# The first loads of a fused attention and MLP kernel: one chunk in two halves, two chunks on another queue, one warming matmul less

## The chip, the cores and the metric

The kernel runs on one core of a Trainium2 chip. A core has five engines that run side by side, each through its own list of instructions, in order: TensorE (PE; its weight loads are shown as PEld), VectorE (DVE), ScalarE (ACT), GpSimd (POOL) and SyncE (SP). They wait for each other by semaphores. Loads and stores are issued by an engine, SP in almost all cases here, and carried out by 16 DMA engines that the core has.

The metric is device time of one execution in microseconds (us). Durations inside the kernel come from a profile of one execution.

## The reference

The reference normalizes the rows of x (2048 tokens by 1024 columns), and adds to x an attention branch and a token-mixing MLP branch. The branch that the kernel starts with is the MLP; it normalizes the already normalized rows once more and mixes over tokens:

```python
def _B_ref(x, w1, b1, w2, b2):
    B, S, D = x.shape
    h = _layernorm(x, axis=-1)
    u = jnp.einsum('bsd,sf->bdf', h, w1) + b1
    u = _gelu(u)
    y = jnp.einsum('bdf,fs->bds', u, w2) + b2
    return (lambda x, *d: x.transpose(*d))(y, 0, 2, 1)
x = A_x
xn = _layernorm(x, axis=-1)
return x + _A_ref(xn, A_wq, A_wk, A_wv, A_wo, A_beta) + _B_ref(xn, B_w1, B_b1, B_w2, B_b2)
```

All inputs are bf16. The attention branch (32 heads, 4 segments with a memory carried from one to the next, and an output projection) is not touched by the change.

## The kernel before

x is cut into 16 chunks of 128 tokens, c=0 to c=15; a chunk is a tile of 128 partitions by 1024 columns (256 KB) in `xin`. w1 is cut the same way by token; of its 3584 columns the first 512 come first, one piece of 128 by 512 (128 KB) for each chunk, in `w1all`.

**Start.** `loads` (L761) issues the loads. POOL sets two small constants; ACT runs one activation (L765) whose only purpose is to have the table of the Gelu function loaded early; then SP issues, in this order: x chunk 0, x chunk 1, w1 piece 0, x chunk 2, x chunk 3, w1 piece 1, x chunk 4, w1 pieces 2 and 3, x chunk 5, w1 pieces 4 and 5, and from there pairs. All loads go through one helper, `dma` (L247), so all have that line in the profile. Its argument `issuer` says which engine issues; in `loads` it is SP for all.

`warm` (L800) has DVE clear a tile and PE multiply it by itself N_WARM = 12 times, with a result that nobody reads; then DVE writes the constants that the statistics need (L810).

**Statistics and first hidden units.** `norm_and_first_hidden` (L813) writes out the order by hand. For each chunk, mean and variance of its rows are found, then 1/sqrt on POOL (`scale`, L899), then `ln_h` (L907) on DVE writes the normalized chunk into `h`, as two halves of 512 columns for the first chunks. Then `early_hidden` (L912) lets PE multiply the chunk with the w1 piece: 8 matmuls of 128x128 by 128x512, for 4 blocks of hidden units and 2 halves of the columns, added up in 8 banks of PSUM over all 16 chunks. In c=0 to c=2 the four matmuls of the first half come first.

The statistics are shared out:

- c=0: DVE, `bn_stats` over columns 0 to 511 (L876), then over 512 to 1023 (L878), then `aggregate` (L885).
- c=1: `stats_halved`: the first half on DVE (L851), the second in two passes on ACT (L853, sum; L855, squares), a small step on POOL (L857), and `aggregate` on DVE.
- even chunks from c=2: two passes of ACT over the whole chunk (L869, L871).
- odd chunks from c=3: DVE, in halves as c=0.

On DVE the order at the start is: both statistics of c=0 and their aggregate, the first-half statistics of c=1, the first half of `ln_h` of c=0, the aggregate of c=1, the second half of `ln_h` of c=0, the first statistics of c=3, both halves of `ln_h` of c=1. On ACT: the two passes over c=1, then those over c=2, c=4 and so on.

**After that.** `hidden` (L982) computes the other 24 blocks of hidden units with 16 matmuls each for two halves, with w1 streamed in; the normalized x is transposed by DMA on the side. Then come attention and the rest of the MLP, in an order that a planner at build time writes out: it keeps a modelled clock for each engine (`fw.now`) and picks what to put on PE next by comparing modelled times of readiness with PE's clock.

**Waits.** Each tile or part has a resource (`Res`) that remembers who wrote and read it last; an operation waits for what it names in `reads` and `writes`. A chunk of x has one resource, `R_xin[c]`. `over_early` (L684) later reuses the space of `xin` and waits for all that read it.

Of the kernel before, what the change touches and what calls it, by code (L numbers as in the profile page):

```python
# [584 lines left out]
class _Kernel:  # L585
# [3 lines left out]
    N_SLOT = 18  # L589
    RESERVE = 60  # L590
    ACT_STATS = (2, 4, 6, 8, 10, 12, 14)
    N_WARM = 12
    C2 = LN_EPS * LN_EPS / (1.0 + LN_EPS)

    def __init__(self, nc, ctx, A_x, A_wq, A_wk, A_wv, A_wo, A_beta, B_w1, B_b1, B_w2, B_b2, out):
# [27 lines left out]
    def alloc(self):  # L623
        nc = self.nc
        a = self.keep = _Arena(nc, self.SB_BASE, self.SB_END)
        self.brow = a.take("brow", [64, P], BF16)
        self.bt = a.take("bt", [P, 64], BF16)
        self.bc = a.take("bc", [P, 64], F32)
        self.beta_sb = a.take("beta_sb", [P, N_HEAD], BF16)
        self.gcol = a.take("gcol", [P, N_HEAD], F32)  # L630
        self.gate = a.take("gate", [P, N_GRP, 2, 4], F32)
        self.eps8 = a.take("eps8", [P, 2, 4], F32)
        self.diag = a.take("diag", [P, 4, VW], F32)
        self.ln_mv = a.take("ln_mv", [P, N_TCH, 2], F32)
        self.ln_t = a.take("ln_t", [P, N_TCH, 4], F32)
        self.ln_r1 = a.take("ln_r1", [P, N_TCH], F32)
        self.ln_r2 = a.take("ln_r2", [P, N_TCH], F32)
        self.mhalf = a.take("mhalf", [P, N_TCH], F32)
        self.vA = [a.take(f"vA{i}", [P, 4, 16, VW], BF16) for i in range(2)]
        self.MZ32 = a.take("MZ32", [P, N_GRP, GW], F32)  # L640
        self.MZbf = a.take("MZbf", [P, N_GRP, GW], BF16)
        self.srec = a.take("srec", [P, 2, 32], F32)
        self.xnT = [a.take(f"xnT{s}", [P, N_DCH, SEG_L], BF16) for s in range(N_SEG)]
        self.gT = a.take("gT", [P, N_FCH, D_MODEL], BF16)
        self.b1c, self.b2c = self.bc[:, 0:32], self.bc[:, 32:64]

        self.R_brow2 = Res("brow2")
        self.R_brow, self.R_bt, self.R_bc = Res("brow"), Res("bt"), Res("bc")
        self.R_beta, self.R_gcol, self.R_gate = Res("beta"), Res("gcol"), Res("gate")
        self.R_eps, self.R_diag, self.R_mhalf = Res("eps8"), Res("diag"), Res("mhalf")  # L650
        self.R_st = [Res(f"st{c}") for c in range(N_TCH)]
        self.R_mean = [Res(f"mean{c}") for c in range(N_TCH)]
        self.R_var = [Res(f"var{c}") for c in range(N_TCH)]
        self.R_rs = [Res(f"rs{c}") for c in range(N_TCH)]
        self.R_r1 = Res("r1")
        self.R_vA = [[Res(f"vA{i}_{c}") for c in range(4)] for i in range(2)]
        self.R_MZ32 = [Res(f"mz32_{g}") for g in range(N_GRP)]
        self.R_MZbf = [Res(f"mzbf_{g}") for g in range(N_GRP)]
        self.R_srec = [Res(f"srec{i}") for i in range(2)]
        self.R_xnT = [Res(f"xnT{c}") for c in range(N_TCH)]  # L660
        self.R_gT = [[Res(f"gT{fc}_{h}") for h in range(2)] for fc in range(N_FCH)]
        self.R_out = [[Res(f"out{c}_{h}") for h in range(2)] for c in range(N_TCH)]

        self.early_base = a.at
        e = _Arena(nc, self.early_base, self.SB_END)
        self.xin = e.take("xin", [P, N_TCH, D_MODEL], BF16)
        self.xn_tmp = [e.take(f"xn_tmp{i}", [P, D_MODEL], BF16) for i in range(4)]
        self.early_end = e.at
        self.h = e.take("h", [P, N_TCH, D_MODEL], BF16)
        self.w1all = e.take("w1all", [P, 3 * N_TCH * 256], BF16)  # L670
        self.ln_st = e.take("ln_st", [P, N_TCH, 15], F32)
        self.late_end = e.at
        self.w1first = self.w1all[:, 0:N_TCH * 512].rearrange("p (c f) -> p c f", c=N_TCH)
        self.w1slot = [self.w1all[:, i * N_TCH * 256:(i + 1) * N_TCH * 256].rearrange("p (c f) -> p c f", c=N_TCH)
                       for i in range(3)]
        self.R_xin = [Res(f"xin{c}") for c in range(N_TCH)]
        self.R_xnt = [Res(f"xnt{i}") for i in range(4)]
        self.R_half = [Res(f"half{i}") for i in range(3)]
        self.R_one = Res("one")
        self.R_h = [[Res(f"h{c}_{hf}") for hf in range(2)] for c in range(N_TCH)]  # L680
        self.R_w1f = [Res(f"w1f{i}") for i in range(N_TCH)]
        self.R_w1s = [None, None, Res("w1s2")]

    def over_early(self):  # L684
        fw = self.fw
        e = _Arena(self.nc, self.early_base, self.early_end)
        wait = _after(*self.R_xin, *self.R_xnt)
        self.wv_sb = e.take("wv_sb", [P, N_DCH, D_MODEL], BF16)
        self.wqr = [e.take(f"wq{i}", [P, N_DCH, P], BF16) for i in range(2)]
        self.wkr = [e.take(f"wk{i}", [P, N_DCH, P], BF16) for i in range(2)]  # L690
        self.w2r = [e.take(f"w2n{i}", [P, 5, P], BF16) for i in range(5)]
        self.w2l = [e.take(f"w2l{i}", [P, 4, P], BF16) for i in range(4)]
        self.w2s = [e.take(f"w2s{i}", [P, P], BF16) for i in range(2)]
        self.prod = e.take("prod", [P, 4, P], BF16)
        self.R_prod = Res("prod", wait)
        self.o_s = [e.take(f"o_s{i}", [P, 4, P], BF16) for i in range(2)]
        self.R_os = [Res(f"o_s{i}", wait) for i in range(2)]
        self.R_wv = [Res(f"wv{i}", wait) for i in range(2)]
        self.R_wq = [Res(f"wq{i}", wait) for i in range(2)]
        self.R_wk = [Res(f"wk{i}", wait) for i in range(2)]  # L700
        self.R_w2 = [Res(f"w2n{i}", wait) for i in range(5)]
        self.R_w2l = [Res(f"w2l{i}", wait) for i in range(4)]
        self.R_w2s = [Res(f"w2s{i}", wait) for i in range(2)]
        self.pkT = e.take("pkT", [P, SEG_L], BF16)
        self.etmp = e.take("etmp", [P, SEG_L], BF16)
        self.R_pkT = Res("pkT", wait)
        self.R_etmp = Res("etmp", wait)
        self.wq_ring = _Ring(fw, [t[:] for t in self.wqr], self.R_wq)
        self.wk_ring = _Ring(fw, [t[:] for t in self.wkr], self.R_wk)
        for i in range(N_UNIT):  # L710
            g = i % N_GRP
            self.wq_ring.srcs.append(self.A_wq[:, g * P:(g + 1) * P].rearrange("(dc p) j -> p dc j", p=P))
            self.wk_ring.srcs.append(self.A_wk[:, g * P:(g + 1) * P].rearrange("(dc p) j -> p dc j", p=P))
        self.fill = _Fill(self)
        self.wq_ring.ensure(0)
        self.wk_ring.ensure(0)
        for bv in range(2):
            fw.dma(self.wv_sb[:, :, bv * 512:(bv + 1) * 512],
                   self.A_wv[:, bv * 512:(bv + 1) * 512].rearrange("(dc p) j -> p dc j", p=P), writes=[self.R_wv[bv]])
# [41 lines left out]
    def loads(self):  # L761
        fw = self.fw
# [1 line left out]
        fw.op("pool", lambda e: e.memset(self.brow[:], 0.0), writes=[self.R_brow, self.R_brow2])  # L764
        fw.op("act", lambda e: e.activation(self.ln_t[:, 0, 0:1], self.mhalf[:, 0:1], ACT.Gelu_apprx_tanh),  # L765
              reads=[self.R_mhalf], writes=[self.R_st[0]], ns=1500)
        self.load_x(0, 1)
        self.load_x(1, 1)
        self.load_w1(0, 1)
        self.load_x(2, 1)  # L770
        self.load_x(3, 1)
        self.load_w1(1, 1)
        self.load_x(4, 1)
        self.load_w1(2, 2)
# [2 lines left out]
        for c in range(6, 16, 2):  # L777
            self.load_x(c, 2)
            self.load_w1(c, 2)
            if c == 6:  # L780
                fw.dma(self.brow[0:N_FCH, :], self.B_b1.rearrange("(c q) -> c q", q=P), reads=[self.R_brow],
                       writes=[self.R_brow])
                fw.dma(self.brow[32:32 + N_TCH, :], self.B_b2.rearrange("(c q) -> c q", q=P), reads=[self.R_brow2],
                       writes=[self.R_brow2])
# [3 lines left out]
        fw.dma(self.w1slot[2], self.w1_srcs[2], writes=[self.R_w1s[2]])  # L788
        self.w1_next = 3

    def load_x(self, c0, n):
        self.fw.dma(self.xin[:, c0:c0 + n, :], self.x_d[:, c0:c0 + n, :],
                    writes=[self.R_xin[c] for c in range(c0, c0 + n)])

    def load_w1(self, c0, n, issuer="sp"):
        self.fw.dma(self.w1first[:, c0:c0 + n, :],
# [63 lines left out]
    def stats(self, c, part=None, whole=True):  # L860
        fw = self.fw
# [13 lines left out]
        if part != 1:  # L875
            fw.op("dve", lambda e: e.bn_stats(st[:, 0:6], src[:, 0:512]), reads=[self.R_xin[c]], writes=[R_t], ns=690)  # L876
        if part != 0:
            fw.op("dve", lambda e: e.bn_stats(st[:, 6:12], src[:, 512:1024]), reads=[self.R_xin[c], R_t], writes=[R_t],  # L878
                  ns=690)
            if whole:  # L880
                self.aggregate(c)
# [20 lines left out]
    def ln_h(self, c, half=None):  # L902
        fw = self.fw
        a, z = (0, D_MODEL) if half is None else (512 * half, 512 * half + 512)
        for hf in ((0, 1) if half is None else (half,)):
            assert self.R_h[c][hf] is not None
        fw.op("dve", lambda e: e.tensor_scalar(self.h[:, c, a:z], self.xin[:, c, a:z], self.ln_mv[:, c, 0:1],  # L907
                                               self.ln_r2[:, c:c + 1], op0=ALU.subtract, op1=ALU.mult),
              reads=[self.R_xin[c], self.R_mean[c], self.R_rs[c]],
              writes=self.R_h[c] if half is None else [self.R_h[c][half]], ns=(z - a) // 2 + 30)  # L910

    def early_hidden(self, c):  # L912
# [51 lines left out]
    def ln_xn(self, c):  # L964
        fw = self.fw
        k = c % 4
        fw.op("dve", lambda e: e.tensor_scalar(self.xn_tmp[k][:], self.xin[:, c, :], self.ln_mv[:, c, 0:1],
                                               self.ln_r1[:, c:c + 1], op0=ALU.subtract, op1=ALU.mult),
              reads=[self.R_xin[c], self.R_mean[c], self.R_r1], writes=[self.R_xnt[k]], ns=750)

    def x_transpose(self, c):
        s, cc = c // 4, c % 4
# [656 lines left out]
```

## Time and profile before

| | us |
|---|---|
| median of 5 runs | 690.8 |
| lowest and highest | 690.37, 690.84 |
| the profiled execution | 690.8 |
| its span, first to last instruction | 689.1 |

Lines of the profile give the start, the duration, the engine, the source line, the operation, `out<-in` by the program's names, shapes, and in brackets how long the engine sat idle before and what ended the wait. "SPq" and "ACTq" are the sequencers of those engines: issuing a load or waiting for a semaphore is their work and not counted as busy time. The early loads and when they land, from the DMA issues of the first 6 us (issue plus time to landing):

| load | issued by SP at | to landing | landed |
|---|---|---|---|
| x chunk 0, 256 KB | 0.81 | 2.8 | 3.6 |
| x chunk 1, 256 KB | 1.26 | 2.9 | 4.2 |
| w1 piece 0, 128 KB | 1.72 | 4.3 | 6.0 |
| x chunk 2, 256 KB | 2.19 | 4.5 | 6.7 |
| x chunk 3, 256 KB | 2.65 | 4.7 | 7.4 |
| w1 piece 1, 128 KB | 3.14 | 4.5 | 7.6 |
| x chunk 4, 256 KB | 3.61 | 4.7 | 8.3 |

### The profile page before, as it was taken

How to read it: one execution, taken by the hardware profiler on the slowest of the kernel's cores; microseconds unless marked ns; L12 is line 12 of the kernel's file. 1: busy time of each engine (PE TensorE's matmuls, PEld its weight loads, DVE VectorE, ACT ScalarE, POOL GpSimd, SP SyncE). 2: the span in 40 equal slices, each digit the busy share in tenths (PEclk: the TensorE clock that was granted, in tenths of full speed). 3: DMA queues.
4: the chain of work that ended last, by engine and by line, in shares of the span. 5: the costliest groups of instructions: out<-in, count | busy, mean ns of one | idle time of the engine just before them, and what ended most of it. 6: DMA issues, size and time to landing. Idle time of an engine off the chain costs nothing.

```text
span 689.1 us, 12060 instructions
## 1 busy us (share of the span) xinstructions
PE 679.4 (99%) x4772; PEld 327.0 (47%) x4853; DVE 235.2 (34%) x510; ACT 308.6 (45%) x611; POOL 150.1 (22%) x363
## 2 busy tenths in 40 slices
PE   8999999999999999999999999999999999999998
PEld 3444444444444454444454544544545444544554
DVE  7811100000001242434462461643536333442524
ACT  7331111111134475755645472744747443534540
POOL 4800000000001232323312231312323131312330
DMA  8367666325027656657547556474564546445334
GB/s 321 109 178 183 159 159 200 100 61 144 1 83 179 148 132 149 146 120 182 132 102 159 124 123 151 94 169 106 130 147 103 120 117 159 107 102 136 86 85 138
DMA packets 275714, 92.06 MB, mean 134 GB/s; under 512 B 234186, under 2 KB 272074, under 8 KB 275658
## 3 DMA queue, kind: packets, MB, share of 16 engines
q1 hardware_dynamic: 275658, 91.28, 53.5%
q8 instruction: 39, 0.64, 0.4%
q14 instruction: 17, 0.14, 0.1%
HBM read 74.47 MB, written 5.24 MB: 116 GB/s over the span
## 4 chain that ended last, share of the span: by engine, by line
PE 96%; DMA 1%; ACT 1%; issue 1%; DVE 0%; SPq 0%
PE ps_all L217 96%; DMA xin<-in_A_x_dram 1%; DMA w2n<-in_B_w_dram 1%; ACT pT L1161 1%; ACT xn_tmp L869 0%; DVE ost L1230 0%; SPq L247 0%; ACT xn_tmp L871 0%; DVE h L907 0%; DVE fin L1368 0%
## 5 line engine op out<-in xcount | busy, mean ns | idle before, releaser
L1169 POOL TENSOR_SCALAR_AFFINE_SELECT pT<-pT 128x256 bf16<-128x256 bf16 (+1 forms) x320 | 127.5, 408 | 508.4 <-ACT pT L1161 498.8
L1161 ACT ACTIVATE pT<-ps_all 128x512 bf16<-128x512 f32 x320 | 161.9, 618 | 76.7 <-PE ps_all L217 76.7
L217 PE MATMUL ps_all<-h,w1all 128*128 128x512 bf16 x878 | 192.9, 379 | 1.7 <-DVE ln_mv L885 0.4
L217 PEld LDWEIGHTS ps_all<-h,w1all 128*128 128x128 bf16 x896 | 87.5, 98 | 107.2 <-issue 1.3
L217 PE MATMUL ps_all<-gT,w2n 128*128 128x512 bf16 x543 | 122.6, 379 | 1.0
L1016 ACT ACTIVATE gT<-ps_all,bc 128x512 bf16<-128x512 f32 x56 | 37.7, 690 | 140.9 <-PE ps_all L217 135.4
L217 PEld LDWEIGHTS ps_all<-gT,w2n 128*128 128x128 bf16 x560 | 54.3, 98 | 64.4 <-DMA w2n<-in_B_w_dram 0.6
L217 PE MATMUL ps_all<-gT,w2l 128*128 128x512 bf16 x300 | 80.3, 380 | 1.7 <-issue 0.8
L1231 ACT ACTIVATE ost<-ps_all 128x264 bf16<-128x264 f32 (+1 forms) x97 | 34.0, 379 | 75.6 <-PE ps_all L217 74.3
L1491 DVE SCALAR_TENSOR_TENSOR stg<-ps_all,bc,stg 128x512 bf16<-128x512 f32 x32 | 23.9, 746 | 125.1 <-PE ps_all L217 125.1
L217 PE MATMUL ps_all<-xnT,wk 128*128 128x512 bf16 x255 | 60.4, 379 | 0.1
L217 PE MATMUL ps_all<-wv_sb,xnT 128*128 128x512 bf16 x252 | 59.8, 379 | 0.2
L217 PE MATMUL ps_all<-xnT,wq 128*128 128x512 bf16 x248 | 58.7, 379 | 0.5
L217 PEld LDWEIGHTS ps_all<-vA,pT 128*128 128x128 bf16 x1280 | 41.3, 96 | 5.0 <-issue 0.6
L217 PEld LDWEIGHTS ps_all<-gT,w2l 128*128 128x128 bf16 x325 | 27.6, 97 | 33.8 <-issue 10.1
L217 PE MATMUL ps_all<-vA,pT 128*128 128x33 bf16 x1280 | 42.8, 177 | 0.0
L954 DVE TENSOR_SCALAR gcol<-gcol 128x32 f32<-128x32 f32 x1 | 0.2, 180 | 118.6 <-ACT gcol L952 118.6
L217 PEld LDWEIGHTS ps_all<-xnT,wk 128*128 128x128 bf16 x256 | 25.1, 98 | 30.2
L217 PEld LDWEIGHTS ps_all<-wv_sb,xnT 128*128 128x128 bf16 x256 | 24.9, 98 | 30.5 <-ACT pT L1161 4.0
L1042 ACT ACTIVATE kT<-ps_all 128x512 bf16<-128x512 f32 x32 | 19.1, 597 | 43.3 <-PE ps_all L217 43.3
L217 PEld LDWEIGHTS ps_all<-xnT,wq 128*128 128x128 bf16 x256 | 23.4, 97 | 29.5 <-issue 6.4
L217 PE MATMUL ps_all<-wo_sb,oT 128*128 128x512 bf16 x124 | 30.5, 379 | 0.3
(78 smaller groups left out, 477.7 us busy)
## 6 DMA issues: line engine op xcount, KB each, us to landing
w2n<-in_B_w_dram SPq DMA_DIRECT2D x100, 160.0 KB, 2.7
w1all<-in_B_w_dram SPq DMA_DIRECT2D x12, 1024.0 KB, 5.2
w2l<-in_B_w_dram SPq DMA_DIRECT2D x73, 128.0 KB, 2.5
wq<-in_A_wq_dram SPq DMA_DIRECT2D x32, 256.0 KB, 2.9
wk<-in_A_wk_dram SPq DMA_DIRECT2D x32, 256.0 KB, 3.4
stg<-in_A_x_dram SPq DMA_DIRECT2D x32, 128.0 KB, 2.8
out_dram<-stg SPq DMA_DIRECT2D x32, 128.0 KB, 2.1
xin<-in_A_x_dram SPq DMA_DIRECT2D x5, 512.0 KB, 7.1
```

Of the source, the lines that this page charges most:

```text
L217: ins = self.nc.tensor.matmul(out, *args, **kwargs)
L954: fw.op("dve", lambda e: e.tensor_scalar(self.gcol[:], self.gcol[:], 1.0, None, op0=ALU.add), reads=[self.R_gcol], writes=[self.R_gcol])
L1016: fw.op("act", lambda e: e.activation(self.gT[:, fc, half * 512:(half + 1) * 512], self.bank(b), ACT.Gelu_apprx_tanh, bias=self.b1c[:, fc: ...
L1042: self.flow.op({"act": (lambda e, b: e.activation(dst, view(self.bank(b)), ACT.Copy), 585, 540), "dve": (lambda e, b: e.tensor_copy(dst, v ...
L1161: fl.op({"act": (lambda e, b, slot=slot: e.activation(pT[:, slot, :], self.bank(b), ACT.Exp, scale=SCALE), 575, 488)}, [], [R[slot]], box= ...
L1169: fl.op({"pool": (lambda e, ap=ap, pat=pat: e.affine_select(ap, ap, pattern=pat, compare_op=ALU.is_ge, fill=0.0, base=0, channel_multiplie ...
L1231: "act": (lambda e, b: e.activation(dst, self.ps[:, b, 0:n * VW], ACT.Copy), 175 + n * 27, 140 + n * 27)},
L1491: engs={"dve": (lambda e, b: e.scalar_tensor_tensor(dst, k.bank(b), k.b2c[:, c:c + 1], dst, op0=ALU.add, op1=ALU.add), 750, 785)},
```

## The change

x chunk 0 is loaded by two DMAs, columns 0 to 511 and 512 to 1023, both issued by SP. The second half has a resource of its own, `R_x0`; the second statistics of c=0, its `ln_h` and the later `ln_xn` wait for it as well, and so does `over_early`. x chunks 2 and 3 are issued by ACT, behind the activation that loads the table. SP's order becomes: both halves of chunk 0, chunk 1, w1 piece 0, w1 piece 1, chunk 4 and on as before. The warming matmuls are 11 instead of 12.

```diff
-    N_WARM = 12
+    N_WARM = 11
...
+        self.R_x0 = Res("x0")
...
-        wait = _after(*self.R_xin, *self.R_xnt)
+        wait = _after(*self.R_xin, self.R_x0, *self.R_xnt)
...
-        self.load_x(0, 1)
+        for half in range(2):
+            cols = slice(512 * half, 512 * half + 512)
+            fw.dma(self.xin[:, 0, cols], self.x_d[:, 0, cols], writes=[self.R_x0 if half else self.R_xin[0]])
         self.load_x(1, 1)
+        self.load_x(2, 1, "act")
         self.load_w1(0, 1)
-        self.load_x(2, 1)
-        self.load_x(3, 1)
+        self.load_x(3, 1, "act")
         self.load_w1(1, 1)
...
-    def load_x(self, c0, n):
+    def load_x(self, c0, n, issuer="sp"):
         self.fw.dma(self.xin[:, c0:c0 + n, :], self.x_d[:, c0:c0 + n, :],
-                    writes=[self.R_xin[c] for c in range(c0, c0 + n)])
+                    writes=[self.R_xin[c] for c in range(c0, c0 + n)], issuer=issuer)
...
-            fw.op("dve", lambda e: e.bn_stats(st[:, 6:12], src[:, 512:1024]), reads=[self.R_xin[c], R_t], writes=[R_t],
+            fw.op("dve", lambda e: e.bn_stats(st[:, 6:12], src[:, 512:1024]), reads=[self.R_x0 if c == 0 else self.R_xin[c], R_t], writes=[R_t],
...
-              reads=[self.R_xin[c], self.R_mean[c], self.R_rs[c]],
+              reads=[self.R_xin[c], self.R_mean[c], self.R_rs[c]] + ([self.R_x0] if c == 0 else []),
...
-              reads=[self.R_xin[c], self.R_mean[c], self.R_r1], writes=[self.R_xnt[k]], ns=750)
+              reads=[self.R_xin[c], self.R_mean[c], self.R_r1] + ([self.R_x0] if c == 0 else []), writes=[self.R_xnt[k]], ns=750)
```

## The prediction

> **What bounds the kernel now.** I read the page first: the span, PE's share and the chain of waits. Then the chain up to 40 us, the timeline of the first 16 us, the landing of each early load, and the bytes moved per stretch.
>
> ```profile
> span 689.1 us, 12060 instructions
> PE 679.4 (99%) x4772; PEld 327.0 (47%) x4853; DVE 235.2 (34%) x510; ACT 308.6 (45%) x611; POOL 150.1 (22%) x363
> PE 96%; DMA 1%; ACT 1%; issue 1%; DVE 0%; SPq 0%
> ```
>
> The chain is PE for 96%. The profiled execution took 690.8 us, 1.7 around the span, and its time equals the median of the five runs, so no correction stands between my sum and that median. All the change can touch is what lies ahead of PE's unbroken run:
>
> ```profile
> 2.19 4.54 DMA xin<-in_A_x_dram
> 6.75 1.16 ACT xn_tmp L869 x2
> 7.93 1.15 ACT xn_tmp L871 x2
> 9.08 1.05 ACT xn_tmp L869 x2
> 10.14 0.42 DVE h L907
> 10.70 4.69 PE ps_all L217 x21
> ```
>
> The columns are start, duration, what. The chain leads from the load of the third chunk (c=2; issued 2.19, landed 6.73) through ACT's two passes over it and the scaling of its first half into PE at 10.70; from there I find no hole above 0.05 us up to 200 us, where I stopped reading the chain. So I count in one number: **when PE starts c=2**. A microsecond there is a microsecond of the span.
>
> ```profile
> 1.25 4.91 PE L217 MATMUL ps_all<-gT 128*128 128x512 bf16 x12 [1.25 <-DVE ln_st L810]
> 4.21 0.63 ACT L853 ACTIVATE xn_tmp<-xin 128x512 bf16<-128x512 bf16 x1 [1.91 <-DMA xin<-in_A_x_dram]
> 6.57 1.42 PEld L217 LDWEIGHTS ps_all<-h,w1all 128*128 128x128 bf16 x8 [0.93 <-DMA w1all<-in_B_w_dram]
> 6.60 3.83 PE L217 MATMUL ps_all<-h,w1all 128*128 128x512 bf16 x16 [0.43 <-DVE ln_mv L885]
> ```
>
> PE warms to 6.16, idles 0.44, does c=0 and c=1, idles 0.26. ACT's passes over x1 run from 4.21 to 5.69 (1.48), then ACT idles 1.06 for x2. Making c=2 earlier needs x2 by about 5.7, x1 no later than now, and c=0 started earlier.
>
> **Where ScalarE's two loads really start.** They stand behind the table load (0.80 to 2.08) and its activation (to 2.30). But a wait that stands behind both was carried out earlier:
>
> ```profile
> L65 ACTq EVENT_SEMAPHORE  x1: 17/17/17, 1.7 to 1.7; - x1
> ```
>
> This is ACT's sequencer at 1.7, waiting for DVE's constants for the x1 passes, while the table load still ran. So the sequencer does not stand still for the table load, and a load issued there can start before 1.7. Bounds for the first issue: 0.85 (as soon as SP's, at 0.81) and 2.30 (after the activation). I take about 1.0, since a sequencer seen ahead of its engine has nothing else to wait for. Then x2 and x3 are moved not behind x0 and x1 but beside them.
>
> **x1's landing.** The stretches show 70 and 111 GB/s in the half microseconds from 1.5 to 2.5, some 90 kB, then 381 and 399. At 390 kB per us, x0 and x1 (524 kB) are moved by 3.6; x1 landed at 4.21, 0.6 behind. Now x0, x1, x2 and x3 (1,049 kB) are in flight together; shared evenly, x1 ends with the last of them: 2.5 + 959/390 = 5.0, plus 0.6 is 5.55. Lower bound: it is only issued one place later, 4.21 + 0.42 (one issue; that of the first w1 load took 0.42) = 4.63. I take 5.55, as the trace moved no more than 400 GB/s while only one queue was filled.
>
> The Trainium skill (DMA: Bandwidth & Descriptors, "Issuing engines are not separate DMA queues") speaks against this change: loads of several issuers share the same 16 engines and interleave, so only issue time is saved. By that rule x1 is at 5.55; were the queues independent, it would be at 4.63 and c=2 would gain. The trace of before has one load queue only and cannot show which.
>
> **Part by part, to the start of c=2.**
> - *ACT's chain.* x1 at 5.55, its passes 1.48: ACT is free at 7.03, by when x2 is there (same sum, about 5.6). Before, the passes over x2 started at 6.75 upon a landing at 6.73. Thus +0.30 against 6.73, and c=2 starts at 11.00. The next chunk's pass on ACT shifts alike, but PE needs c=4 only at about 14.2, with ACT done with it at 11.3 before.
> - *x0 in halves.* One more issue on SP, +0.42 for x1 and the first w1 load. The first half lands by the same sum at 2.5 + 172/390 + 0.6 = 3.5, if one half and as many bytes of x2 go first; the second at 4.2 (524 kB). The statistics (0.69 and 0.68) end at 4.9 instead of 5.02: 0.1 gained. Bounds: 0.35 if the halves land undisturbed, -0.6 if x2 and x3 both go ahead of the second half. Either is lost, since behind them on DVE stands x1's first-half pass (L851, 0.64), now waiting for x1 until 5.55, and the scaling of c=0 (L907) is queued behind it: 6.2 instead of 6.04. It is late by 0.15, and its second half waits behind L885, which needs ACT's passes: about 7.1 to 7.5.
> - *First w1 load.* By the sum for 655 kB it would have landed at 4.55; it landed at 6.0 (issue 1.72, 4.3 to landing). It lagged 1.5. Now it ends at 1,180 kB: 5.9 without a lag, 7.4 with. c=0 starts between 6.65 and 7.45; 16 matmuls at 0.215 to 0.24 end at 10.5 to 11.2. PE then meets c=2's data at 11.0 or up to 0.2 later.
> - *One warming matmul less.* Covered: PE idles from 6.16 to 6.60 anyway. If c=0 could start before 6.16 it would be worth up to 0.29.
> - *Issues.* Two loads leave SP and one is added: x4 and all behind it are issued some 0.45 earlier. Worth nothing: the engines move 385 GB/s from 6.6 on, and the bytes ahead of x4 are the same. ACT's issues (0.43 each by SP's rows) lie in its idle 1.91 before 4.21; with that cover gone they would cost 0.9.
> - *Later order.* The order in attention is planned from modelled times relative to PE; early loads are long past. Nothing, unless rounding flips a choice; I leave 0.2 for that.
>
> Sum: +0.30, 690.8 + 0.3 = **691.1**; its own range 690.6 to 691.9.
>
> **Rivals.**
> *A. The loads do wait for the table load* (the change does as its name says). x1 at 4.63 to 5.0, ACT free by 6.1 to 6.5. x2, issued at about 2.3, lands on a queue of its own ahead of its old 6.73. c=0 is held by the first w1 load (6.0 + 0.42 = 6.42), c=1 ends near 10.3: c=2 at 10.35, -0.35, 690.4; at best -0.7. For: the diff's order. Against: the wait at 1.7.
> *B. The clock is not released by 11 matmuls.* Place: c=0 and c=1.
>
> ```profile
> L217 PE MATMUL ps_all<-gT 128*128 128x512 bf16 x10 | 4.4, 628 | 1.3 <-DVE ln_st L810 1.3
> L217 PE MATMUL ps_all<-gT 128*128 128x512 bf16 x2 | 0.7, 417 | 0.0
> ```
>
> Ten warming matmuls take 628 ns each at a pitch of 0.43, the last two 417, later ones 379 at 0.215. The column of the granted clock says 1.00 throughout, so only durations show it: release came at about 5.65, in the eleventh, 4.4 us after the first matmul. With eleven, PE is still busy then, but by only 0.15. Missed, c=0 and c=1 run at 0.43 until 4.4 us of new work are done: 10 matmuls to 11.0, 6 more to 12.3, and c=2 starts at 12.4: +1.4 over the forecast, 692.5. It decides from a release later than the last warming matmul. For: the idle after warming grows from 0.44 to at least 0.9. Against: five runs within 0.5 us.
> The Trainium skill (TensorE: Matmul & The Clock Gate, Part 1) has the release come at the end of a free-running window of about 3.4 us, so its phase could differ from run to run. By that length instead of 4.4, c=0 and c=1 would run 8 matmuls slow to 10.0 and end at 11.7, and the price would be an estimated 0.75 instead of 1.4.
> *C. x1 itself lags.* By my sum x2 should have landed at 5.2 and came at 6.73: some engines ran 1.5 behind. If that belongs to the time after 4 us and not to the w1 load, x1 gets it: 7.05, c=2 at 12.5, 692.6. It counts beyond 0.2% from x1 at 6.6. Against: x1 had no lag, and the first w1 load, the first that lagged, still stands behind x1.
>
> **How the numbers follow.** Forecast 0.50; A 0.24; B 0.12; C 0.12; anything else 0.02. 0.2% is 1.4 us, about what a measurement of this kernel can tell from no change. The forecast and A lie within it, except for edges: faster 0.03 (A beyond its best end, a better later order). Slower 0.22: nearly all of B and C. Within: 0.75. The range for 8 in 10 takes in A to -0.7 and most of B and C: 690.1 to 692.5.
>
> **What would show it.** Right: ACT's queue issues x2 and x3 before 1.7; x1 lands at 5.2 to 5.8; ACT starts x2 without idling; c=2 starts on PE at 10.8 to 11.3; the rest is as long as before. A: issues after 2.1, x1 below 5. B: matmuls of c=0 at a pitch of 0.43. C: x1 beyond 6.6. I am wrong altogether if PE's run after c=2 changes by more than 0.3 us, or if arbitration between the queues isn't even.

## The result and the profile after

| | before | changed |
|---|---|---|
| median, us | 690.39 (51 runs) | 691.35 (30 runs) |
| lowest and highest | 689.78, 691.11 | 690.91, 694.08 |
| the profiled execution | 690.8 | 691.06 |
| its span | 689.1 | 689.3 |

The ratio is 1.0016, with a 95% interval of 1.0011 to 1.0021: the change makes the kernel some 1.0 us slower. The ratio itself is below the 0.2% that the prediction took as its bound for no change, but over 81 runs it is a loss and not noise.

The chain of waits of the changed kernel in its first 17 us (start, duration, what):

```profile
1.72 4.09 DMA xin<-in_A_x_dram
5.81 0.02 issue
5.84 0.73 ACT xn_tmp L856 x2
6.57 0.02 issue
6.59 0.72 ACT xn_tmp L858 x2
7.31 1.05 ACT xn_tmp L872 x2
8.36 0.02 issue
8.38 1.15 ACT xn_tmp L874 x2
9.54 1.05 ACT xn_tmp L872 x2
10.58 0.01 issue
10.59 0.43 DVE h L910
11.02 0.14 issue
11.15 4.91 PE ps_all L217 x22
```

The lines are three further down than before (L853 is now L856, L869 is L872). Before, the chain came from x chunk 2, which ACT waited for; now it comes from chunk 1: issued at 1.72, landed at 5.81 instead of 4.19, and ACT goes from its passes over chunk 1 (L856, L858) to those over chunk 2 (L872) without a pause. c=2 starts on PE at 11.15 instead of 10.70.

The timeline of the changed kernel shows why chunk 1 is late:

```profile
0.80 1.28 ACT L766 ACT_TABLE_LOAD   x1 [0.80 <-PEq L1617]
0.81 1.34 SPq L247 DMA_DIRECT2D xin<-in_A_x_dram  x3
0.95 0.86 ACTq L247 DMA_DIRECT2D xin<-in_A_x_dram  x2
1.25 3.92 PE L217 MATMUL ps_all<-gT 128*128 128x512 bf16 x11 [1.25 <-DVE ln_st L813]
5.84 0.63 ACT L856 ACTIVATE xn_tmp<-xin 128x512 bf16<-128x512 bf16 x1 [3.54 <-DMA xin<-in_A_x_dram]
6.99 3.86 PE L217 MATMUL ps_all<-h,w1all 128*128 128x512 bf16 x16 [1.81 <-DVE h L910]
```

ACT's sequencer issues chunks 2 and 3 from 0.95 to 1.81, in the middle of the table load (0.80 to 2.08) that they stand behind in the program. SP issues the two halves of chunk 0 and then chunk 1 at 1.72, as the last of the five. ACT, which idled 1.91 us for chunk 1 before, idles 3.54 now, and PE waits 1.81 between its warming and c=0 instead of 0.43.

The five engines of the profiled executions carry out the same work in the same order as before, but for the two issues that moved, the added one and the missing matmul; beside that only a few waits for semaphores differ. So nothing was replanned.

### The profile page after: what moved, and what is told of

The parts are those of the page before. It is cut to its first block, busy times and chain, and to the rows that moved or that the text cites. A ratio compares the mean times of both kernels' runs of the same rounds, so it can differ in the third digit from the quotient of the medians.

```text
span 689.3 us, 12060 instructions
## 1 busy us (share of the span) xinstructions
PE 678.4 (98%) x4771; PEld 326.5 (47%) x4852; DVE 235.1 (34%) x510; ACT 308.4 (45%) x611; POOL 150.4 (22%) x363
## 4 chain that ended last, share of the span: by engine, by line
PE 97%; ACT 1%; issue 1%; DMA 1%; DVE 0%; SPq 0%
PE ps_all L217 97%; DMA xin<-in_A_x_dram 1%; ACT pT L1164 1%; ACT xn_tmp L872 0%; DVE ost L1233 0%; ACT xn_tmp L874 0%; SPq L247 0%; ACT xn_tmp L856 0%; ACT xn_tmp L858 0%; DVE h L910 0%; DVE fin L1371 0%
```

## The experiments

Two theories stood after the result. Theory 1: the loss is the late start of c=2, and that comes from chunk 1, which lands when chunks 2 and 3 on the other queue have been moved too. Theory 2 takes up rival B: the clock of PE, which eleven matmuls and a longer idle stretch do not bring up in every execution. The halves of chunk 0 were a third suspect (rival H). "Pitch" is the time from the start of one matmul to the start of the next; 0.43 is the long pitch of the first warming matmuls, 0.215 the short one. Each kernel was timed against the kernel before on the same chip.

**One part alone: eleven warming matmuls.**

```diff
-    N_WARM = 12
+    N_WARM = 11
```

> The kernel before with 11 warming matmuls instead of 12, nothing else. Theory 1 (the start of c=2 decides, and it follows x1's landing on ACT; warming plays no part): c=2 starts as in before, 10.4 to 10.8, time 690.4, within 0.2 of before. Rival B (eleven matmuls do not release the clock in time in many executions): some or most executions run c=0 and c=1 at a pitch of 0.43, time 690.9 to 692.4, at least 0.5 over before.

690.41 against 690.40, ratio 1.0001 (0.9992 to 1.0010). In a kernel whose c=0 comes at 6.7, no worth of the twelfth matmul can be seen. In the profile all eleven matmuls kept the long pitch, to 6.13, and c=0 began at the short one 0.54 later. So eleven matmuls alone cost nothing that could be measured; the longer idle stretch of the changed kernel is not tested by this.

**One part alone: the two loads on ACT's queue.**

```diff
-        self.load_w1(0, 1)
-        self.load_x(2, 1)
-        self.load_x(3, 1)
+        self.load_x(2, 1, "act")
+        self.load_w1(0, 1)
+        self.load_x(3, 1, "act")
```

> The kernel before with x chunks 2 and 3 issued by ACT, chunk 0 whole, 12 warming matmuls. Theory 1: the loads are issued at 0.95 and 1.4, x1 lands at 5.2 to 5.8 instead of 4.2, ACT goes from x1 to x2 without idling, c=2 starts at 10.7 to 11.2, and the time is the whole of the change's loss or nearly so: 690.9 to 691.5. Rival B: at most half of the loss, 690.4 to 690.8, the rest is the warming matmul's. Rival H (splitting chunk 0 costs, since it puts one more issue ahead of x1): under 690.7 as well.

690.87 against 690.40, ratio 1.0010 (1.0001 to 1.0019): by the medians half of the loss, between what theory 1 and rival B expected, and the interval reaches from nearly none of it to all of it. Chunk 1 landed at 5.4 and c=2 started at 10.75, both inside the stretches that theory 1 stated. The profiled execution took 690.64 and was the second fastest of the eleven; two others took 692.5, with 12 warming matmuls. The chain of waits leads through chunk 0 here. These are its pieces up to its aggregate:

```profile
0.81 3.38 DMA xin<-in_A_x_dram
4.18 0.02 issue
4.21 0.71 DVE ln_st L876
4.91 0.02 issue
4.93 0.70 DVE ln_st L878
5.64 0.02 issue
5.66 0.23 DVE ln_mv L885
```

Chunk 0, issued first of all, landed at 4.18 instead of 3.6, with chunk 2 moved beside it, and the statistics of c=0 were late; c=0 started at 7.18. So the second queue takes from every load that PE needs first, not from chunk 1 alone. The chain counts PE as busy from there on, but c=2 itself was set by chunk 1 and ACT:

```profile
5.44 0.63 ACT L853 ACTIVATE xn_tmp<-xin 128x512 bf16<-128x512 bf16 x1 [3.14 <-DMA xin<-in_A_x_dram]
10.19 0.74 DVE L907 TENSOR_SCALAR h<-xin,ln_mv,ln_r 128x512 bf16<-128x512 bf16 x2 [0.59 <-ACT xn_tmp L869]
```

DVE stood idle for ACT's passes and scaled the first half of c=2 from 10.19 to 10.60; PE started it 0.15 later, as in the changed kernel (11.00 and 11.15). At the short pitch PE would have been free at 10.63.

**One part alone: the halves of chunk 0**, all on SP, in the order of before, with 12 warming matmuls.

> The kernel before with chunk 0 in two halves on SP's queue, everything else as before, 12 warming matmuls. Theory 1: the first half lands 0.3 earlier, x1 is issued one place later and lands at 4.3 to 4.7, x2 is what ACT waits for, so c=2 stays at 10.4 to 11.0 and the time within 0.3 of before, 690.2 to 690.7. Rival H: x1 and all behind it 0.45 later, c=2 at 11.1 or later, 690.8 or more.

690.76 against 690.40, ratio 1.0006 (0.9997 to 1.0015): not clear of no change, and just between what theory 1 and rival H expected. In its profile the halves landed at 3.1 and 3.5, c=0 started at 6.16 instead of 6.60, and chunk 1 landed at 4.75. c=2 still started at 10.79: chunk 3 landed only at 7.89 in this execution, and c=1 waited for the statistics of chunk 3 that stand ahead of it on DVE. A gain at c=0 was lost at the next wait.

**ACT's loads held behind the activation, as rival A had it.**

```diff
-        self.load_x(2, 1, "act")
+        self.load_x(2, 1, "act", [self.R_st[0].w])
```

> The changed kernel, but the first load on ACT's queue waits for the activation behind the table load (chunk 2 issued at 2.3 or later, chunk 3 behind it). This is what the change's name says. Theory 1: x0 and x1 have the engines to themselves, x1 lands at 4.6 to 5.0, ACT is free at 6.1 to 6.5, x2 has landed by then, c=2 starts at 10.2 to 10.7: 689.9 to 690.5, at least 0.5 under the changed kernel and not above before. Rival B: the loss stays, 690.9 or more, since there are still 11 warming matmuls. Rival A's price of the prediction, 0.35 under before, is tested too.

690.58 against 690.40, ratio 1.0001 (0.9992 to 1.0010). No loss can be seen with this one wait, although the halves and the 11 warming matmuls are still there: neither they nor rival H can be the whole of it. But the gain of rival A did not come. Chunk 1 landed at 5.44, not at 4.6 to 5.0, although chunk 2 was issued only at 2.33. The bytes moved in the held kernel, per half microsecond (the last two columns are the DMA engines' busy share and GB/s):

```profile
2.50:3.00 0.50, 0.50 (x3) 0.22 (x2) 0.00 (x0) 0.00 (x0) 0.00 (x0) 1.00 1.98 268
3.00:3.50 0.50, 0.50 (x3) 0.23 (x2) 0.48 (x1) 0.00 (x0) 0.00 (x0) 1.00 0.34 66
3.50:4.00 0.50, 0.50 (x3) 0.17 (x2) 0.40 (x2) 0.00 (x0) 0.00 (x0) 1.00 0.00 0
4.00:4.50 0.50, 0.50 (x2) 0.15 (x1) 0.50 (x1) 0.00 (x0) 0.00 (x0) 1.00 0.56 217
```

Behind the two halves hardly a packet started for a microsecond, and from 3.5 to 4.0 none at all. What stopped them was not found. So this profile does not show what rival A would be worth without that gap.

**Half the dose: only chunk 2 on ACT's queue.**

```diff
         self.load_w1(0, 1)
-        self.load_x(3, 1, "act")
+        self.load_x(3, 1)
```

> The changed kernel with only chunk 2 on ACT's queue, chunk 3 back on SP's behind the first w1 load. Theory 1 (x1 lands when all that is in flight with it has been moved): 786 kB instead of 1,049 kB, so x1 lands at 4.7 to 5.2 instead of 5.8, ACT is free at 6.2 to 6.7, c=2 starts at 10.1 to 10.6, and the time is 0.4 to 0.9 under the changed kernel: 690.2 to 690.8. Rival (what costs is that ACT issues at all, or the halves): 690.9 or more.

690.48 against 690.58, ratio 1.0003 (0.9994 to 1.0011): with 256 KB less ahead of chunk 1 no loss can be seen, as theory 1 says. But the one profile fell on an execution of 692.74, the slowest of the eleven, and showed rival B; the landing at 4.7 to 5.2 that theory 1 stated was not seen. Chunk 1 landed at 5.96, of which more below, and then:

```profile
1.25 4.87 PE L217 MATMUL ps_all<-gT 128*128 128x512 bf16 x11 [1.25 <-DVE ln_st L813]
7.14 6.13 PE L217 MATMUL ps_all<-h,w1all 128*128 128x512 bf16 x20 [1.01 <-DVE h L910]
```

Eleven warming matmuls took 4.87 here and 3.92 in the changed kernel's profile, where the last four ran at the short pitch. Here none did; PE idled 1.0, and c=0 began at 7.14 at the long pitch. c=2 started at 12.25.

**The changed kernel with 16 warming matmuls.**

```diff
-    N_WARM = 11
+    N_WARM = 16
```

> The changed kernel with 16 warming matmuls instead of 11, so that PE works on until about 6.0 to 6.9, shortly before c=0. Theory 1: c=2 still starts behind ACT's passes over x1 and x2, at 10.8 to 11.3, median 691.0 to 691.5 as the changed kernel. Theory 2 (a part of the executions, those at 692.1 and more with a granted clock of 0.998, loses time because PE idles 2 us between warming and c=0 and the clock is taken back or not yet given): those executions are gone, none above 691.8 in eleven, median within 0.15 of the changed kernel's 691.35. Rival B, if it were the whole loss: median 690.4 to 690.7.

691.13 against 690.58, ratio 1.0008 (0.9999 to 1.0017): 0.55 between the medians, but not clear of no change. The highest of eleven is 691.80; the changed kernel had five of thirty at 692.1 or more, and three of them show a granted clock of 0.998. c=2 started at 10.95, and the chain runs through chunk 1 (5.62), ACT's passes and DVE as in the changed kernel. So the chain behind the loss stays with more warming. The tail was not met, but in the changed kernel's two sets only 7 of 41 executions took 691.9 or more, and at that rate eleven without one would come by chance about one time in eight.

**The changed kernel once more.**

> The changed kernel once more, on the same chip as the next three. Theory 1: x1 lands behind x2 and x3 at 5.4 to 6.0, c=2 starts at 10.9 to 11.4, time 690.9 to 691.5, 0.5 to 1.0 over before on this chip. Theory 2 (the clock is not released by eleven matmuls in some executions): one to three of some eleven executions at 692 or more, and a profile that falls on one shows c=0 and c=1 at a pitch of 0.43.

691.02 against 690.34, ratio 1.0015 (1.0006 to 1.0024). Two of eleven executions lay at 691.9 and 692.0, and the profile fell on one of those. In the stretch from 7 to 10 us, the groups of PE's matmuls here (count, busy time, mean ns of one):

```profile
L217 PE MATMUL ps_all<-h,w1all 128*128 128x512 bf16 x8 | 3.5, 620 | 0.9 <-DVE h L910 0.9
```

and in the changed kernel's first profile:

```profile
L217 PE MATMUL ps_all<-h,w1all 128*128 128x512 bf16 x13 | 3.2, 379 | 1.8 <-DVE h L910 1.8
```

8 matmuls at 620 ns against 13 at 379, with chunk 1 at 5.86 and 5.81: the same loads, but matmuls at the long pitch. c=2 started at 12.13, 0.98 later than in the first profile, and the execution took 0.92 longer.

**The kernel before once more.**

> The kernel before once more, for a second profile. If its executions differ by how long some engines lag behind the first w1 load, this profile shows another landing of x2 than 6.73, and c=2 moves with it one for one as far as 10.05, where PE's own work on c=0 and c=1 holds it: 689.8 to 691.1.

690.54 against 690.58. Its profile (690.43) has chunk 2 at 5.32 instead of 6.73, and c=2 at 10.43 instead of 10.70. Not one for one: now PE's own c=0 and c=1 and the chain to c=1 hold it. So the executions of the kernel before differ by how late single loads come, and the one that the prediction was worked from was a late one. With 11 warming matmuls and the same loads, chunk 2 came late too, at 6.80.

**A version for the cause: chunk 2 ahead of the first w1 load, SP alone.**

```diff
-        self.load_w1(0, 1)
         self.load_x(2, 1)
+        self.load_w1(0, 1)
         self.load_x(3, 1)
```

> The kernel before with SP issuing x chunk 2 ahead of the first w1 load: x0, x1, x2, w1 piece 0, x3; nothing on ACT. Theory 1 with the lag (some engines run up to 1.5 behind from the first w1 load on, and what is queued behind it lands late): x2 lands at 4.8 to 5.4 instead of 5.2 to 6.8, ACT goes on to it at 5.7, c=2 is held by PE at 10.0 to 10.4, times close together at 689.8 to 690.2, median 0.2 to 0.5 under before. Rival (the lag belongs to the time after 4 us, whatever is loaded): x2 still lands beyond 6 in the profile and the median stays within 0.15 of before; or the w1 piece, one place later, holds c=0 beyond 7 and the median is 0.2 or more over before.

689.90 against 690.58, ratio 0.9991 (0.9982 to 1.0000). A second time, on another chip:

> The kernel before with x chunk 2 ahead of the first w1 load, a second time. Theory 1: 0.4 to 0.7 under before, close together, none above 690.5, c=2 at 10.0 to 10.3, since ACT no longer waits for a lagging x2. Rival (the first result was chance, its interval just touched no change): within 0.2 of before.

690.08 against 690.34, ratio 0.9996 (0.9987 to 1.0004). In the chain of the second profile ACT is gone; what leads to c=0 is chunk 0 and its statistics, and from 6.47 PE does not stop:

```profile
5.91 0.24 DVE h L907
6.15 0.09 issue
6.24 0.23 DVE ln_mv L885
6.46 0.00 issue
6.47 6.63 PE ps_all L217 x30
```

c=2 started at 10.06 and 9.92. The medians lie 0.7 and 0.3 under the kernel before, where 0.4 to 0.7 was expected the second time; both intervals touch no change, and the second run had one of eleven above 690.5. So a gain of a few tenths is likely and not shown. On the second chip it lies 0.9 under the changed kernel (690.08 and 691.02).

**The halves added to it.**

> The kernel before with chunk 0 in two halves on SP and chunk 2 ahead of the first w1 load. Theory 1: the halves let c=0 start at 6.1 to 6.3 if the w1 piece, now issued fifth, is there, but x1 is issued one place later and ACT's chain from x1 (5.45 from its landing to c=2) sets c=2 at 10.0 to 10.5: no gain over the same kernel with chunk 0 whole, 689.9 to 690.4. Rival (c=0's start decides): 0.2 or more under it.

690.28 against 690.34, ratio 1.0002 (0.9993 to 1.0011). As theory 1 said: c=0 started at 6.30, chunk 1 landed at 5.12, ACT's chain set c=2 at 10.45.

**Chunk 1 instead of 2 and 3 on ACT's queue, with chunk 2 ahead of the first w1 load.**

```diff
-        self.load_x(1, 1)
+        self.load_x(1, 1, "act")
+        self.load_x(2, 1)
         self.load_w1(0, 1)
-        self.load_x(2, 1)
```

> The kernel before with x chunk 1 alone on ACT's queue, issued at 0.95, and SP's order x0, x2, w1 piece 0, x3. Theory 1: loads land about in the order of their issue over both queues, so x1 lands at 3.9 to 4.3, x2 by 5.0, the w1 piece half a microsecond earlier than with SP alone; c=2 is held by PE's work from c=0 at 6.5: 10.0 to 10.2, time 0.4 to 0.8 under before, equal to or up to 0.2 under the kernel with x2 first on SP. Rival (a second queue costs by itself, by delaying x0): x0 lands at 4.0 or later, c=0 at 6.9 or later, time not under before.

690.23 against 690.34, ratio 0.9998 (0.9989 to 1.0006): the rival's side. Chunk 0 landed at 3.97, c=0 started at 6.98, and c=2 at 10.43 with no hole on PE before it. Even one load on the other queue, issued 0.14 after the first, delays the first by some 0.4: with SP alone chunk 0 landed at 3.46 to 3.65 in five profiles, with a load on ACT at 0.95 at 3.97 and 4.18. Its first half alone landed at 2.98 to 3.07 in three profiles without an early load on ACT, and at 3.28 to 3.57 in four with one.

All profiles in one table. The start of c=2 is the start of the seventeenth matmul behind the warming ones; "rest" is the time of that execution less that start.

| kernel | chunk 1 landed | c=2 | time | rest |
|---|---|---|---|---|
| before | 4.2 | 10.70 | 690.80 | 680.1 |
| before, again | 4.2 | 10.43 | 690.43 | 680.0 |
| 11 warming matmuls | 4.3 | 10.76 | 691.08 | 680.3 |
| ACT loads alone | 5.4 | 10.75 | 690.64 | 679.9 |
| halves alone | 4.8 | 10.79 | 690.93 | 680.1 |
| ACT loads held | 5.4 | 10.77 | 690.67 | 679.9 |
| changed | 5.8 | 11.15 | 691.06 | 679.9 |
| changed, 16 warming | 5.6 | 10.95 | 690.80 | 679.9 |
| changed, again | 5.9 | 12.13 | 691.98 | 679.9 |
| chunk 2 alone on ACT | 6.0 | 12.25 | 692.74 | 680.5 |
| chunk 2 first | 4.1 | 10.06 | 690.33 | 680.3 |
| chunk 2 first, again | 4.3 | 9.92 | 690.38 | 680.5 |
| halves, chunk 2 first | 5.1 | 10.45 | 690.28 | 679.8 |
| chunk 1 on ACT | 4.6 | 10.43 | 690.29 | 679.9 |

The rest stays within 679.8 to 680.5 while c=2 moves by 2.3: nearly all that a kernel does to the time it does ahead of c=2. But the 0.7 by which the rest varies is as large as most differences here, which is why single executions say little and the verdicts go by medians. A part of it can be placed: in the four executions with a rest of 680.3 or more, PE stopped once more, for 0.26 to 0.37, at 371 or at 416 to 418 us, for a load of w2 (`w2n`). Both profiles with chunk 2 first are among them, so what they gained at c=2 did not all arrive in the time.

One number ties chunk 1 to c=2. In the five profiles in which c=2 was ready last by ACT's chain from chunk 1 (ACT loads alone, ACT loads held, changed, changed with 16 warming, halves with chunk 2 first), c=2 started 5.33 or 5.34 after chunk 1 had landed, with landings from 5.12 to 5.81. In the others c=2 came later than that, held by another load or by PE itself.

## Why the prediction was right, and where it was off

- **Where ACT's loads start** (about 1.0, from the wait that ACT's sequencer carried out at 1.7 during the table load): 0.95 and 1.37. Right, and the step on which the sign hung: held behind the activation (2.33), the same loads cost nothing that could be measured.
- **x1 at 5.55, all four chunks in flight together**: 5.81, 5.86 and 5.62 in the three profiles of this order, 0.1 to 0.3 later. That x1 lands behind the bytes of all four chunks is right; that they share evenly is not, and the prediction had named uneven sharing as a sign that it is wrong altogether. In the changed kernel's profile the loads landed at 3.4 (first half of chunk 0), 4.0 (chunk 2), 4.3 (second half), 5.0 (chunk 3), 5.8 (chunk 1): in the order of their issue, over both queues. From 2.5 to 4.5 ACT's queue (q10) moved nearly three times the bytes of SP's (queue, kind, packets, MB, share):

```profile
q10 hardware_dynamic: 280, 0.52, 73.3%
q1 hardware_dynamic: 190, 0.19, 28.2%
```

The sum held all the same, because x1 was issued last of the four and so landed behind all their bytes. By even sharing the place in the order would not have mattered; that x1 was last is luck for this sum. With chunk 0 whole the queues moved more alike (0.51 and 0.41 MB from 3.0 to 5.5), but the order shows again: chunk 1, issued at 1.25 ahead of chunk 3 (1.37), landed at 5.42 and chunk 3 at 6.13. So the halves count after all: they move chunk 1's issue behind chunk 3's. In the profiles that is worth 0.40 at c=2 (11.15 against 10.75). In the medians the two kernels' intervals overlap, so that the parts together cost more than the two loads alone is likely and not shown.

- **c=2 at 11.00**: 11.15. Against the profile of before that it was worked from, the forecast was +0.30 and 0.45 was measured. The rest behind it, 679.9 against 680.1, stayed within the 0.3 that the prediction allowed.
- **+0.3 in time**: +0.96 between the medians. The term that was mis-sized is the base, "no correction stands between my sum and that median". The five runs shown (690.8) lay above the 690.39 of 51, and the profiled execution had chunk 2 at 6.73; a second one had it at 5.32 and c=2 at 10.43. Counted from there, the changed kernel's c=2 is 0.72 later; and its profiled execution, 691.06, lay 0.29 under its median. So the forecast of 691.1 came within 0.25 of the median of 691.35 by luck: a base 0.4 too high made up for a difference 0.66 too small.
- **The halves' own gain (0.1), lost behind x1's pass on DVE**: the halves landed at 3.4 and 4.3 (predicted 3.5 and 4.2), the aggregate of c=0 was at 5.06 against 5.07, and the scaling of c=0 at 6.45 against 6.04, behind L854 as predicted (6.2).
- **The first w1 load, 5.9 without a lag, 7.4 with**: 6.15. It did not hold c=0.
- **One warming matmul less, covered**: right for the kernel before. For the changed one, where PE idles 0.9 to 1.8 ahead of c=0, it is open: two of the eleven executions with ACT's loads alone took 692.5 with 12 warming matmuls, and both show a granted clock of 0.998. So a tail comes without the missing matmul too. PE idles longer ahead of c=0 in both kernels (0.63 with ACT's loads alone, 0.43 before), which fits rival B's place but was not tested by itself. Rival B was priced at c=2 = 12.4; the two profiles that fell on it show 12.13 and 12.25. It was put as all or nothing. In the changed kernel's two sets of runs it can account for at most 7 of 41 executions (691.9 or more); one of these has a profile, and the highest, 694.08, lies beyond rival B's price and was not explained. It makes a tail, not the median.
- **Rival A, -0.35**: tested by holding the loads; no gain came (1.0001). Its price took it that chunk 1 would land by 5.0, and it landed at 5.44.
- **Rival C and the lag**: the lag was put down to the first w1 load, and that step was wrong. In the second profile of before that load did not lag (4.64) and chunk 3 behind it did (7.52); with chunk 2 alone on ACT, chunk 1 itself came at 5.96 where 8 of the 16 signals of its landing had come by 4.63 and the last three came at 5.93 and after, ahead of any w1 load. Some of the 16 parts of a load fall behind in some executions; why stays open.

## What to carry to other kernels

In these runs a load put on a second queue did not wait its turn behind what the first queue held, and it did not wait for the engine work in front of it either: it landed by the time of its issue, and the loads under way at that time landed later. Where the DMA engines are already moving all they can, order the loads by who waits for them first, on one queue if need be, and give a load a wait of its own if it has to stay behind another. Read which wait ends last from the start of the matmul and the end of what fed it: the chain of waits can pass over a hold of a tenth of a microsecond. Where the warming of PE is trimmed, look at the stretch between the last warming matmul and the first real one as well, not at the number of matmuls alone.

## What the runs showed of the hardware

- The release of the clock, taken from the change of pitch from 0.43 to 0.215, came at about 4.1 in the changed kernel's first profile, 5.65 in the before's, and at 10.4 and 10.5 in the two that missed it, with the first matmul at 1.25 in all. The column of the granted clock read 1.00 in each of these profiles. In two others no warming matmul had the short pitch (to 6.13 with 11, to 6.55 with 12 and ACT's loads), and c=0 still began at it, 0.54 and 0.63 later; the two that missed it idled 0.9 and 1.0.
- Issues from ACT and SP at the same time (0.95 to 1.81 and 0.81 to 2.15) took 0.38 to 0.45 each, as SP's alone before (0.39 to 0.43): two queues issued at twice the rate. Up to 6.0 us the highest rate in half a microsecond stayed where it was, 399 GB/s before and 400 in the changed kernel, but the rest was fuller: from 1.5 to 6.0, 1.39 MB were moved against 1.21 before.
- After the two halves the first packets of the next load took long: 0.5 with the halves alone and 1.1 to 1.3 in the held kernel, in which no packet started from 3.5 to 4.0. Packets of the first load of all took up to 0.6 in some profiles too, with chunk 0 whole.
